# The last 16 columns of V in five loads by rows: a cached attention decode step with a gated mixer MLP

## Chip, cores and metric

The kernel runs on one core of one Trainium2 chip. The metric is device microseconds of one execution of the program: the median of several runs. The profile shows one more execution, taken with the hardware profiler.

## What is computed

Two branches start from the same input x (2 batches, one token, 1024 features), and a gate g = sigmoid(sum(x * gate_w)) mixes them.

```python
# A: one token against a cache of 16384 keys and values, 32 heads of 128
q = (x @ wq)                                     # (2, 32, 1, 128)
scores = einsum("bhqd,bhkd->bhqk", q, k_cache) * (128 ** -0.5)
o = einsum("bhqk,bhkd->bhqd", softmax(scores), v_cache)
a = o.reshape(2, 1, 4096) @ wo
# B: h = gelu(layernorm(x) @ w1), shifted along the sequence, @ w2;
#    x1 = x + hs;  b = x1 + gelu(layernorm(x1) @ w3) @ w4
out = g * a + (1 - g) * b                        # (2, 1, 1024), bf16
```

Everything is bf16 in memory. K and V are 268 MB each, the weights some 36 MB more.

## The kernel before

**Units.** The 32 heads of a batch are taken in 16 pairs, one pair of one batch is a unit, and there are 32 units: `i` counts the pairs, `s` the batches. A unit's K (and later its V) is 8 MB and lies in SBUF as 128 rows of 64 KB: row p holds 256 consecutive cache positions ("columns" of 128 values each, `NJ` = 256), and the first 64 rows belong to one head, the last 64 to the other. `unit_rows` gives that view of the cache in HBM.

**One unit.** POOL spreads the unit's query (L624). DVE transposes the K data in eight chunks (L640), and PE multiplies each with the query (L663) into PSUM. DVE takes the maximum (L647, L649), ACT exponentiates (L685) into `pts`, and PE sums (L704). For the unit before, PE multiplies V with its `pts` (L713, `pv_moving`, 512 values of V at a time moving through PE), DVE adds and scales the parts (L781, L787, `dve_rows`), PE turns them (L731), and after each pair of units PE projects with eight of Wo's slices (L758, `add_rows`).

**Order.** The engines' orders and the semaphores are written out by hand in one critical section. SP issues every large load, all on one queue (q1 in the profile): in the loop K of the unit (L906) when the DVE has transposed enough of the unit before in that cell, V of the unit before (L908) when PE has finished with the V cell, and Wo for a pair (L911). Each `dma_start` raises its semaphore by 16 when it has landed. ACT issues three small loads of four rows each at the start (x and the gate's weights, L82) and the store of the result at the end (L1017), on queue q10.

**The end.** After the loop two units of V remain. SP issues V of the first of them (L934) when the last K data of cell 0 are transposed, and, when PE is done with the V cell, V of the second (L938) in pieces of 128, 64, 48 and 16 columns (`PIECES`), each over all 128 rows. Behind them come the Wo rows of the last two heads in three loads (L946 to L948). PE multiplies the first 192 columns with `pv_moving`; DVE adds the parts; PE puts the result into `last` (L992). The other 64 columns are multiplied the other way round, one column of V at a time as PE's weights and two columns of `pts` moving (L996), piece by piece, with a wait for each piece ahead of its first matmul. DVE scales the sum (L1002), PE projects it with Wo (L758, twelve matmuls, then a wait for the load of L948, then four more), ACT and DVE copy the two halves out of PSUM (L1013, L1015), and ACT stores them (L1017).

The waits that the change touches: the semaphores of these loads were used once before at the kernel's start, so each starts at 16, and `landing(n)` is the value that means that piece n has landed:

```python
for n in range(WIDE, len(PIECES)):
    wait(PE, landed[n + 1], landing(n + 1))
    for _ in range(PIECES[n]):
        ins = PE.matmul(last, lhsT=V[:, j, :], rhs=pts[1][:, j // 4, :, j % 4], ...)
        j += 1
```

Of the kernel before, what the change touches and what calls it, by code (L numbers as in the profile page):

```python
# [88 lines left out]
def kernel(  # L89
# [16 lines left out]
    P = nc.NUM_PARTITIONS  # L106
    B, Sq, D = A_x.shape
    _, H, Sk, Dh = A_k_cache.shape
# [6 lines left out]
    HP = H // 2  # L115
    HALF = P // 2
    NJ = 2 * Sk // P
# [4 lines left out]
    Q4 = 4  # L122
# [19 lines left out]
    def S(name):  # L142
        if name not in sems:
            sems[name] = (tc if name in ("fin", "st") else nc).alloc_semaphore(name)
        return sems[name]
# [59 lines left out]
    def region(cell, elements):  # L205
        return mem[:, cell * CELL : cell * CELL + elements]

    K_CELL = (0, 1)
    V_CELL = 3

    k_rows = A_k_cache.rearrange("b (g t) s d -> b g (t s d)", t=2)
    v_rows = A_v_cache.rearrange("b (g t) s d -> b g (t s d)", t=2)
    wo_rows = A_wo.rearrange("(g p r) n -> g (p r n)", p=WP, r=WR)

    def unit_rows(rows, hp, s):
        if isinstance(hp, int):
            flat = rows[s, hp : hp + 1, :]
        else:
            flat = rows[s, bass.ds(hp, 1), :]
        return flat.rearrange("o (p x) -> (o p) x", p=P)  # L220
# [7 lines left out]
    def wait(engine, name, value):  # L228
        if isinstance(value, int) and value == 0:
            return  # L230
        engine.wait_ge(S(name), value)
# [7 lines left out]
    with tc.tile_critical(no_gpsimd_drain=True):  # L239
        PE, DVE, ACT, POOL, SP = nc.tensor, nc.vector, nc.scalar, nc.gpsimd, nc.sync  # L240
# [10 lines left out]
        for b, row in enumerate((A_x[0, 0], A_x[1, 0], gate_w)):  # L251
# [9 lines left out]
                out=ident_f[:], in_=ident_f[:], compare_op=ALU.not_equal, fill=1.0, base=0,  # L261
# [10 lines left out]
        for k in range(2):  # L272
# [14 lines left out]
                out=lmat[:].rearrange("p (g h k) -> p g h k", h=2, k=4),  # L287
                in_=hm2[:].unsqueeze(1).unsqueeze(3).to_broadcast([P, P // 8, 2, 4]),
# [3 lines left out]
        for h in range(2):  # L292
            at = QP + h * (HB // 2)
# [3 lines left out]
                    out=place[:, at : at + P].rearrange("p (g k) -> p g k", k=2 * QP)[:, :, 0 : HB + 1 : HB],  # L297
                    in_=ident_f[:, h * HALF : (h + 1) * HALF].rearrange("p (g k) -> p g k", k=QP)[:, :, 0:B],
# [6 lines left out]
                out=ident_s[:], in0=ident_f[:], scalar1=-scale, scalar2=None, op0=ALU.mult  # L305
# [6 lines left out]
                out=rep1[:], in_=ident_f[:].rearrange("p (c k) -> p k c", k=QP), axis=AX.X, op=ALU.add  # L312
# [6 lines left out]
                out=mask4[:], in_=ident_f[:].rearrange("p (c k) -> p c k", k=QP), axis=AX.X, op=ALU.add  # L319
# [3 lines left out]
        for g in range(Q4):  # L323
# [3 lines left out]
                    out=rep4[:, g, :].rearrange("p (a k) -> p a k", k=QP),  # L327
# [13 lines left out]
                out=hsel[:], in_=rep1[:, 0:8].rearrange("p (h k) -> p h k", k=4), axis=AX.X, op=ALU.add  # L341
# [179 lines left out]
        def linear(actT, w, R, N, act_key, w_key, banks, out_keys):  # L521
# [7 lines left out]
            def one(n):  # L529
# [19 lines left out]
                out=tsc[:],  # L549
                in_=oacc2[:].rearrange("p a (m k e) -> p (a m) e k", k=QP, e=2),  # L550
# [6 lines left out]
                out=qTb[:], in_=tsc[:].rearrange("p (c k) -> p c k", k=QP)[:, :, 0:B]  # L557
# [15 lines left out]
        for e in range(2):  # L573
# [4 lines left out]
                    out=qd[rows],  # L578
                    in_=R_ps[rows].rearrange("p (hp e v b) -> p e hp b v", e=2, v=4, b=B)[:, e],
# [142 lines left out]
        def v_view(cell):  # L722
            return region(cell, NJ * Dh).rearrange("p (j d) -> p j d", d=Dh)
# [105 lines left out]
        for key in ("qd", "mask4", "qw0", "qw1"):  # L829
# [20 lines left out]
                out=tsc[:, 0:FQ],  # L850
                in_=oacc2[:, :, 0:half].rearrange("p a (i c) -> p c a i", c=FC),
# [34 lines left out]
                out=brow[:], in0=brow[:], scalar1=omgrow[:, 0:1], scalar2=None, op0=ALU.mult  # L886
# [38 lines left out]

        landed = [f"l_{x}" for x in ("wq", "w1", "w2", "xr0", "xr1", "w3", "w4")]

        def landing(n):
            return 32

        PIECES = [128, 64, 48, 16]
        WIDE = 2
        wait(SP, "tr3", 2 * HP)
        SP.dma_start(out=region(0, NJ * Dh), in_=unit_rows(v_rows, HP - 1, 0)).then_inc(S(landed[0]), 16)  # L934
        wait(SP, "pvd", 2 * HP - 1)
        at = 0
        for n, size in enumerate(PIECES):
            SP.dma_start(  # L938
                out=region(V_CELL, NJ * Dh)[:, at * Dh : (at + size) * Dh],
                in_=unit_rows(v_rows, HP - 1, 1)[:, at * Dh : (at + size) * Dh],  # L940
            ).then_inc(S(landed[n + 1]), 16)
            at += size
        wo_heads = A_wo.rearrange("(h d) n -> d h n", d=Dh)
        wo_l = region(2, 2 * D).rearrange("p (e n) -> p e n", e=2)
# [20 lines left out]
                out=rinv2[:], in0=rinv2[:], scalar1=g_rep[:, 1:2], scalar2=None, op0=ALU.mult  # L965
# [14 lines left out]
        V = v_view(V_CELL)  # L980
        moving = sum(PIECES[:WIDE])
        j = 0
        for n in range(WIDE):
            wait(PE, landed[n + 1], landing(n + 1))
            ins = pv_moving(V, 1, j // 4, (j + PIECES[n]) // 4, moving // 4)
            j += PIECES[n]
# [5 lines left out]
        PE.matmul(last, lhsT=red[:, 0, :], rhs=hsel[:], start=True, stop=False)  # L992
# [3 lines that stand above are left out]
                ins = PE.matmul(  # L996
                    last, lhsT=V[:, j, :], rhs=pts[1][:, j // 4, :, j % 4], start=False, stop=(j == NJ - 1)
                )
                j += 1
        ins.then_inc(S("otd"), 1)  # L1000
        wait(DVE, "otd", 2 * HP)
        DVE.tensor_tensor(out=OTl[:, :, HB], in0=last, in1=rinv2[:], op=ALU.mult).then_inc(S("OTd"), 1)  # L1002
        wait(PE, "OTd", 2 * HP)
        wait(PE, landed[-2], landing(-2))
        for h in range(2):
            add_rows(0, OTl, wo_l, h)
# [11 lines left out]
            out=out.rearrange("b s (h g c) -> g (b s) h c", h=2, g=Q4), in_=out_row[0 : P - HB + 1 : HB, :]  # L1018
# [37 lines left out]
```

## Time and profile before

| what | value |
| --- | --- |
| median of 3 runs | 1331.68 us (1331.62 to 1331.88) |
| the profiled execution | 1331.36 us |
| its span in the profile | 1329.6 us |
| granted TensorE clock, mean | 0.803 |
| DMA traffic | 572.68 MB, 431 GB/s over the span |
| PE busy | 826.6 us (62%) |
| DVE busy | 711.4 us (54%) |
| ACT busy | 105.2 us (8%) |

The span runs from the first instruction to the last; the time of the execution is some 2 us longer. PE and DVE are busy for a good half of the span, spread evenly over it; the sixteen DMA engines are busy throughout. Times within the execution are microseconds from the span's start. The loads of the end are issued like this: L934 at 1277.84, the four pieces of L938 from 1294.34 on (1.76 us of SP for the four), then L946 at 1296.15, L947 at 1296.62 and L948 at 1297.10. Each lands some 20 to 30 us after its issue, since all that was issued before it on the queue comes first. A load's bytes are moved as packets, one for a contiguous run of one row, and the trace has a record of each packet (queue, size, start and duration), and of each increment of a load's semaphore.

### The profile page before, as it was taken

How to read it: one execution, taken by the hardware profiler on the slowest of the kernel's cores; microseconds unless marked ns; L12 is line 12 of the kernel's file. 1: busy time of each engine (PE TensorE's matmuls, PEld its weight loads, DVE VectorE, ACT ScalarE, POOL GpSimd, SP SyncE). 2: the span in 40 equal slices, each digit the busy share in tenths (PEclk: the TensorE clock that was granted, in tenths of full speed). 3: DMA queues.
4: the chain of work that ended last, by engine and by line, in shares of the span. 5: the costliest groups of instructions: out<-in, count | busy, mean ns of one | idle time of the engine just before them, and what ended most of it. 6: DMA issues, size and time to landing. Idle time of an engine off the chain costs nothing.

```text
span 1329.6 us, 14078 instructions
## 1 busy us (share of the span) xinstructions
PE 826.6 (62%) x6060; PEld 378.3 (28%) x6060; DVE 711.4 (54%) x712; ACT 105.2 (8%) x165; POOL 15.9 (1%) x47
## 2 busy tenths in 40 slices
PE   2356576565666656567665657656566775656765
PEld 0123232232332323233232323223232322323323
DVE  2365465654556654456565455665455656545561
ACT  0010000000000000000000000000000000000000
POOL 0100000000000000000000000000000000000000
PEclk9677887777888777788877788877788887778886
DMA  9999999999999999999999999999999999999998
GB/s 410 439 420 436 443 426 440 428 430 436 432 436 432 436 430 442 426 442 426 442 426 442 424 442 426 442 426 433 434 430 438 430 436 432 440 428 440 428 440 346
DMA packets 11573, 572.68 MB, mean 431 GB/s; under 512 B 1472, under 2 KB 1740, under 8 KB 1996
## 3 DMA queue, kind: packets, MB, share of 16 engines
q1 hardware_dynamic: 11520, 572.53, 99.6%
q8 instruction: 8, 0.13, 0.0%
q10 hardware_dynamic: 44, 0.01, 0.0%
q14 instruction: 1, 0.01, 0.0%
HBM read 572.53 MB, written 0.00 MB: 431 GB/s over the span
## 4 chain that ended last, share of the span: by engine, by line
DMA 68%; DVE 14%; PE 13%; issue 3%; another core or an unknown queue 1%; POOL 0%; SPq 0%; POOLq 0%; ACT 0%
DMA mem<-in_A_k_cache_dram 66%; DVE kt L640 14%; PE S L663 12%; DMA mem<-in_A_v_cache_dram 2%; PE oacc L713 0%; PE ot L531 0%; SPq L906 0%; PE R L996 0%; POOL qw L267 0%; POOL pt L269 0%; SPq L938 0%; PE arow L758 0%; DVE st L647 0%; POOL ln_rstd L471 0%
## 5 line engine op out<-in xcount | busy, mean ns | idle before, releaser
L663 PE MATMUL S<-kt,qw 128*128 128x512 bf16 x2048 | 552.1, 420 | 261.7 <-DVE kt L640 261.4
L640 DVE STREAM_TRANSPOSE kt<-mem 128x2048 f32<-128x2048 f32 x256 | 571.6, 2284 | 171.1 <-DMA mem<-in_A_k_cache_dram 115.6
L663 PEld LDWEIGHTS S<-kt,qw 128*128 128x128 bf16 x2048 | 197.9, 105 | 602.1 <-issue 301.3
L713 PE MATMUL oacc<-mem,pt 128*8 128x512 bf16 x2032 | 118.3, 386 | 5.7 <-DMA mem<-in_A_v_cache_dram 5.7
L685 ACT ACTIVATE pt<-st,nb 64x256 bf16<-64x256 f32 x64 | 90.1, 1407 | 279.0 <-DVE nb L699 278.5
L731 PE MATMUL ot<-hsel,red 128*128 128x2 f32 x480 | 71.1, 279 | 54.7 <-DVE red L787 54.7
L731 PEld LDWEIGHTS ot<-hsel,red 128*128 128x128 f32 x480 | 68.5, 224 | 69.9 <-DVE red L787 69.9
L781 DVE TENSOR_SCALAR part<-oacc,maskr 128x128 f32<-128x128 f32 x31 | 10.9, 351 | 140.3 <-PE oacc L713 140.3
L674 ACT ACTIVATE Dm<-ident_s,m 128x128 f32<-128x128 f32 x32 | 12.8, 401 | 878.7 <-DVE m L649 878.7
L704 PE MATMUL R<-rs,lmat 128*128 128x1 f32 x64 | 18.4, 357 | 79.1 <-ACT pt L685 79.1
L713 PEld LDWEIGHTS oacc<-mem,pt 128*8 128x8 bf16 x2032 | 46.9, 87 | 64.8 <-DMA mem<-in_A_v_cache_dram 6.8
L708 DVE RECIPROCAL rinv<-R 128x1 f32<-128x1 f32 x32 | 5.4, 168 | 109.6 <-PE R L704 109.5
L647 DVE STREAM_TRANSPOSE st<-S 128x512 f32<-128x512 f32 x32 | 22.9, 717 | 70.1 <-PE S L663 70.1
L676 PE MATMUL R<-Dm,ones_f 128*128 128x128 f32 x64 | 15.6, 326 | 54.4 <-ACT Dm L674 54.4
L814 DVE TENSOR_SCALAR oa<-ot,hm 128x8 f32<-128x8 f32 x30 | 6.8, 226 | 73.9 <-PE ot L731 73.9
L704 PEld LDWEIGHTS R<-rs,lmat 128*128 128x128 f32 x64 | 15.9, 307 | 84.9 <-ACT pt L685 84.7
L758 PE MATMUL arow<-wo,OT 128*17 128x128 bf16 x960 | 28.3, 310 | 10.5 <-DVE OT L819 10.5
L685 ACT ACTIVATION_READ_ACCUMULATOR pt<-st,nb 64x1 f32 x64 | 30.7, 479 | 0.0
L676 PEld LDWEIGHTS R<-Dm,ones_f 128*128 128x128 f32 x64 | 9.5, 188 | 70.3 <-ACT Dm L674 70.3
L758 PEld LDWEIGHTS arow<-wo,OT 128*17 128x17 bf16 x960 | 24.6, 133 | 11.3 <-issue 11.3
L787 DVE SCALAR_TENSOR_TENSOR part<-oacc,maskr,part 128x128 f32<-128x128 f32 x62 | 21.8, 351 | 2.2
L624 POOL TENSOR_TENSOR qw<-qd,mask 128x16 bf16<-128x16 f32 (+1 forms) x32 | 8.3, 262 | 1118.7 <-PE S L663 1118.7
(114 smaller groups left out, 130.0 us busy)
## 6 DMA issues: line engine op xcount, KB each, us to landing
mem<-in_B_w_dram SPq DMA_DIRECT2D x2, 7168.0 KB, 34.4
wo<-in_A_wo_dram SPq DMA_DIRECT2D x15, 512.0 KB, 24.8
mem<-in_B_w_dram SPq DMA_DIRECT2D x2, 2048.0 KB, 28.5
mem<-in_A_v_cache_dram SPq DMA_DIRECT2D x1, 4096.0 KB, 20.8
mem<-in_A_v_cache_dram SPq DMA_DIRECT2D x1, 2048.0 KB, 25.3
mem<-in_A_v_cache_dram SPq DMA_DIRECT2D x1, 1536.0 KB
mem<-in_A_k_cache_dram SPq DMA_DIRECT2D x32, 28.3
mem<-in_A_v_cache_dram SPq DMA_DIRECT2D x1, 512.0 KB
```

The lines of the kernel that those rows point to most:

```text
L640: DVE.transpose(out=kt[n % 2][:], in_=k_view(s)[:, c * CT : (c + 1) * CT, :].rearrange("p j d -> p (j d)").bitcast(FP32),).then_inc(S(f"tr ...
L647: DVE.transpose(out=st[:].rearrange("p j r -> p (j r)"), in_=sps[s][:]).then_inc(S("stT"), 1)
L663: ins = PE.matmul(sps[s][:].rearrange("p (j k) -> p j k", k=QP), lhsT=qw[s][:, v, NG - 1 - m : NG - 1 - m + P], rhs=ktb[:, half * GT : (ha ...
L674: ACT.activation(out=Dm[:], in_=ident_s[:], func=ACTF.Copy, scale=m_t[:, 0:1]).then_inc(S("dm"), 1)
L676: PE.matmul(R_ps[:, 0:P], lhsT=ones_f[:], rhs=Dm[:], start=True, stop=True).then_inc(S("rr"), 1)
L685: ins = ACT.activation(out=pts[s][rows, :, e, :].rearrange("p (m a) k -> p a k m", a=GT // 4), in_=st[rows, :, 0:NG].rearrange("p (a k) m ...
L704: PE.matmul(tot_ps[:, 0:1], lhsT=lmat[:], rhs=rs_t[:], start=True, stop=True).then_inc(S("tt"), 1)
L713: ins = PE.matmul(oacc[s][QP * q : QP * q + 8, :], lhsT=pts[s][:, g].rearrange("p h k -> p (h k)"), rhs=V[:, 4 * g : 4 * g + 4, :].rearran ...
L731: ins = PE.matmul(ot_ps[:, 2 * r : 2 * r + 2], lhsT=red_t[:, r : r + 2 * P - 1 : 2], rhs=hsel[:], start=True, stop=True, skip_group_check= ...
L758: ins = PE.matmul(arow[h][QP * g : QP * g + HB + 1, :], lhsT=o[:, e, :], rhs=w[:, e, at : at + Dh], start=False, stop=stop, skip_group_che ...
L781: ins = DVE.tensor_scalar(out=part[:], in0=in0, scalar1=mask[:, 0:1], scalar2=None, op0=ALU.mult)
L787: ins = DVE.scalar_tensor_tensor(out=red[:] if twice else part[:], in0=in0.unsqueeze(1).to_broadcast([P, 2, Dh]) if twice else in0, scalar ...
```

## The change

The first three pieces of the last unit's V stay as they are. The last piece, 16 columns (4 KB in each row), is no longer one load of 128 rows: it is one load of rows 0 to 111, then four loads of four rows each, 112 to 115, 116 to 119, 120 to 123 and 124 to 127. All five raise the same semaphore, and the wait on PE for this piece asks for 16 * (2 + 4) = 96 instead of 32. The order of the instructions on PE, DVE, ACT and POOL is the same in both kernels; on SP one load has become five, at the same place, with three loads of Wo behind them.

```diff
-        def landing(n):
-            return 32
-
         PIECES = [128, 64, 48, 16]
         WIDE = 2
+        LAST, FEW = len(PIECES) - 1, 4
+        def landing(n):
+            return 16 * (2 + Q4) if n == LAST + 1 else 32
+
         wait(SP, "tr3", 2 * HP)
         SP.dma_start(out=region(0, NJ * Dh), in_=unit_rows(v_rows, HP - 1, 0)).then_inc(S(landed[0]), 16)
         wait(SP, "pvd", 2 * HP - 1)
         at = 0
         for n, size in enumerate(PIECES):
-            SP.dma_start(
-                out=region(V_CELL, NJ * Dh)[:, at * Dh : (at + size) * Dh],
-                in_=unit_rows(v_rows, HP - 1, 1)[:, at * Dh : (at + size) * Dh],
-            ).then_inc(S(landed[n + 1]), 16)
+            cuts = [0] + (list(range(P - Q4 * FEW, P, FEW)) if n == LAST else []) + [P]
+            for first, end in zip(cuts, cuts[1:]):
+                SP.dma_start(
+                    out=region(V_CELL, NJ * Dh)[first:end, at * Dh : (at + size) * Dh],
+                    in_=unit_rows(v_rows, HP - 1, 1)[first:end, at * Dh : (at + size) * Dh],
+                ).then_inc(S(landed[n + 1]), 16)
             at += size
```

## The prediction

> **What bounds the kernel now.** I read the page first. Its busy row of the DMA engines is full in every slice but the last, and the chain that ended last is mostly transfers.
>
> ```profile
> DMA  9999999999999999999999999999999999999998
> ...
> DMA 68%; DVE 14%; PE 13%; issue 3%; another core or an unknown queue 1%; POOL 0%; SPq 0%; POOLq 0%; ACT 0%
> ```
>
> So the kernel streams 572.7 MB at the rate of its sixteen DMA engines. A change to the last load can matter only where that stream runs out, so next comes the timeline of the last 6 us (columns: start, duration, engine, line, operation; in brackets the idle time and what ended it).
>
> ```profile
> 1323.76 1.86 PE L996 MATMUL R<-pt,mem 128*128 128x2 bf16 x64 [0.32 <-DMA mem<-in_A_v_cache_dram]
> 1325.66 0.17 DVE L1002 TENSOR_TENSOR OT_last<-R,rinv_last 128x2 bf16<-128x2 f32 x1 [2.86 <-PE R L996]
> 1325.89 0.22 PEld L758 LDWEIGHTS arow<-mem,OT_last 128*17 128x17 bf16 x12 [0.34 <-DVE OT_last L1002]
> 1325.89 0.72 PE L758 MATMUL arow<-mem,OT_last 128*17 128x128 bf16 x16 [0.26 <-DVE OT_last L1002]
> 1326.32 0.10 PEld L758 LDWEIGHTS arow<-mem,OT_last 128*17 128x17 bf16 x4 [0.21 <-DMA mem<-in_A_wo_dram]
> 1326.44 0.28 ACT L1013 ACTIVATE out_row<-arow 113x128 bf16<-113x128 f32 x1 [24.48 <-PE arow L758]
> ```
>
> Two paths meet at 1326.32. The chain of waits follows one: the 48-column piece of V lands at 1323.72, PE does its 48 and then 16 one-column matmuls (L996) without a gap, DVE scales, PE starts the projection (L758). The other is the last wait, 0.21 us: the last four matmuls wait for the last quarter of Wo (L948). That wait ends last. If it were gone, the four could start at 1326.11, so a gain can be at most **0.21 us**; a delay of L948's landing costs its whole length.
>
> L948 is behind the changed load in the same queue (SP's, q1). The trace keeps, for each load, the times of its sixteen increments, one by each DMA engine. L948's run from 1324.53 to 1326.28: eight engines are done by 1324.84, eight only from 1325.57 on. The windows say the same (the last two columns are DMA share and GB/s).
>
> ```profile
> 1323.00:1324.00 1.00, 0.69 (x11) 0.60 (x12) 0.00 (x0) 0.00 (x0) 0.00 (x0) 0.50 1.02 386
> 1324.00:1325.00 1.00, 1.00 (x44) 1.00 (x41) 0.00 (x0) 0.00 (x0) 0.00 (x0) 0.50 0.56 208
> 1325.00:1326.00 1.00, 0.74 (x32) 0.66 (x29) 0.17 (x1) 0.00 (x0) 0.00 (x0) 0.50 0.36 117
> ```
>
> The reader is to see a stream that ends ragged: full until 1324, half idle after. What counts is the engine that ends last, and the change gives some engines more and others less.
>
> **Which engine is late.** Each engine takes its own packets of q1 one after another, so its lag on the earliest engine can be followed from load to load: within about 0.1 us it stays, except where the engine also carries an instruction fetch (in q8, 16 KB of 948 to 1164 ns each; the first, at 39.24 us, is 8 KB of q14). Seven fetches between 39 and 196 us hit seven different engines, and one at 1310.39 an eighth. At the 64-column piece the lags are 0 to 0.42 us for eight engines and 1.20, 1.48, 1.55, 1.65, 1.71, 1.72, 1.79 and 1.96 us for the others.
>
> **The change, part by part.** *Removed:* a load of 128 rows of 4 KB: eight rows and one increment on each engine. The 128 packets of 4 KB took 159 to 172 ns, median 160. *Added:* 112 rows, which I take as seven per engine, and four loads of four rows. That a four-row load goes to four engines, one row each, is in the trace: ACT's three four-row loads at the start (x and the gate's weights) left 24 packets, 12 rows and 12 increments.
>
> ```profile
> q10 hardware_dynamic: 24, 0.01, 0.1%
> ```
>
> In those records the four engines stand 0, 0.113, 0.268 and 0.286 us apart in each of the three loads, so all three went to the same four. So four engines get 7+4 = 11 rows and five increments, twelve get 7 rows and one.
> - Twelve engines: one row less, **-0.16 us** each.
> - Four engines: 3 x 0.160 + 4 x 0.01 (an increment took 9 ns, the next packet starts about a nanosecond or two later) = **+0.52 us** each.
>
> Are those four early or late ones? The offsets above fit one set of four in the first loads; followed to the end they stand at about 0.23, 0.24, 1.20 and 1.48 us. The first, second and third become 0.75, 0.76 and 1.72, the fourth 1.48 + 0.52 = 2.00. The latest now, 1.96, is not among them and becomes 1.80. The last lag goes from 1.96 to 2.00: **+0.04 us** at L948's landing and so at the end. The weak step is the fourth: near 52 us three engines cross within 12 ns, and it may be its neighbour at 1.55 (then +0.11) or an early one (then the last is 1.80, -0.16).
>
> *Issue on SP.* L938 has four issues more, 0.43 us each and 0.04 between: 4 x 0.47 = 1.9 us, so the three Wo loads (L946 to L948) are issued from 1298.0 instead of 1296.15. Queue q1 has V to move until 1325, which hides this; without that cover it would cost the 1.9 us. Nothing of POOL or ACT is moved past, and SP issues nothing afterwards. If q1 took fewer loads at once than the twelve now outstanding (eight before), SP would stand until the earlier V load lands at 1305.41, still 20 us ahead of need.
>
> *The wait on PE* for the last piece now asks for 96 instead of 32 (16 old, 16 and four times 16 new). Behind it stand 16 matmuls of L996, then DVE's scaling and the projection. The piece landed at 1324.97 and is needed after 48 matmuls of 29 ns, at 1325.16; 0.04 us more stays inside these 0.19. Nothing else on any engine moves: instructions of PE, DVE, ACT and POOL stand in the same order.
>
> **Sum.** The profiled run took 1331.36 us with a span of 1329.6; +0.04 gives 1331.4 for it. It lies 0.3 below the median of the shown runs, 1331.68, so the forecast is 1331.68 + 0.04 = **1331.7 us**: no change that can be seen.
>
> **A price no row shows: four engines writing four neighbouring rows.** Bounds from rows: Wo's 32-row loads in the loop, two rows per engine, had 16 KB packets of 611 to 622 ns, those of 128-row loads 611 at the start: a change of the rows' pattern cost at most 2%, nothing here. From the other side, if the four engines wrote one after another, each row would take four times 160 ns: 4 x 3 x 0.16 = +1.92 us. I take the first, since it is the nearer operation, and since the four are not in step (0.2, 0.2, 1.2, 1.5).
> The Trainium skill, page "SBUF — State Buffer", section "Door 1: The DMA port swizzle", speaks against the change here: four partitions such as 112 to 115 share one port, and bandwidth depends on how many ports are reached. By that rule the sum would be the upper bound; the 611 to 622 ns do not show it, but no load here writes four neighbouring rows alone.
>
> **Rivals.**
> 1. *The extra rows fall on early engines only.* Then the latest lose a row: -0.16 us, 1331.5. For it: half of the engines are early, and two of the four surely so. Against: the third and fourth as followed.
> 2. *The small loads hinder each other.* Pairs in step (the third and fourth are 0.28 us apart, about two rows) would double the four rows' time on a late engine: 0.04 + 4 x 0.16 = +0.68, 1332.4; all four in turn, +1.96, 1333.6. Against: the 611 to 622 ns above.
> 3. *Each small load pays its own round trip in series* (the case on the other side). The only small transfer with both ends in the trace, the 4 KB store, is issued at 1326.98 and lands at 1328.70: 1.72 us. Four in series on the late engine: 6.9 us in place of 0.64, so +6.3, **1338 us**. It decides as soon as an engine waits for the increment of one load before the next one's row: beyond 1326.11 all of it is on the path. Against: the three Wo loads end 0.34 and 0.32 us apart on the last engine, which leaves no room for 1.7 each, and an increment's packet is followed by the next load's packet at once. The Trainium skill, page "DMA: Bandwidth & Descriptors", section "Anatomy of one DMA — SWDGE (gpsimd) path", gives about 2.0 us fixed per DMA, mostly the write's receipt; as an estimate from it four in series would be 8 us. It was fitted on another issuing path, and the 0.34 us apart speak against it in a full queue.
> 4. *It doesn't do what it says:* a four-row load is cut over all sixteen engines. Then the sum of rows is eight for each as before, with four increments more: +0.04, 1331.7, which the time can't tell from the forecast.
>
> **Chances.** Forecast with rival 4: 0.50 (1331.7). Rival 1: 0.25 (1331.5). Rival 2: 0.14 (1332.4 to 1333.6). Rival 3: 0.10 (about 1338). What would be faster by more than the 0.21 us bound has no mechanism here; 0.01. About 0.2% (2.7 us) is what a measurement of this kernel can tell from no change: only rival 3 passes it. So faster 0.01, same 0.89, slower 0.10. The range leaves out rival 3 and the upper half of rival 2. Below it goes to 1331.68 - 0.21, less some 0.3 for the spread of the runs (1331.36 to 1331.88): 1331.1; above to 1332.4 plus the same: 1332.7.
>
> **What would show it.** Right: L996 still 64 matmuls without a gap; sixteen increments of L948 with twelve of them 0.16 us earlier against the 48-column piece and four 0.5 later, the last within 0.2 of before; the wait before the last four of L758 between 0 and 0.4 us. Wrong: a gap inside L996 or a wait of over 1 us for Wo (rival 3), 4 KB packets well over 172 ns (rival 2), a four-row load with other than four rows' packets and four increments (rival 4). An instruction fetch that hits another engine than before would move the lags by 1 us and spoil the sum without being the change's doing.

## The result

The changed kernel takes 1333.41 us (median of 22 runs, 1333.04 to 1334.41) against 1331.63 us (22 runs, 1331.35 to 1331.97): 1.78 us slower, a ratio of 1.0014 (95% interval 1.0008 to 1.0020, which leaves out 1). The prediction's 1331.7 us and its range up to 1332.7 are both below this. The profiled execution has a span of 1331.6 us, 2.0 more than before.

The loss arises in the last 10 us. First the timeline of the changed kernel from the last one-column matmuls on (start, duration, engine, line, operation; in brackets the idle time and what ended it; L999 and L1005 are L996 and L1002 of before).

```profile
1325.36 1.44 PE L999 MATMUL R<-pt,mem 128*128 128x2 bf16 x48 [0.98 <-DMA mem<-in_A_v_cache_dram]
1327.21 0.59 PE L999 MATMUL R<-pt,mem 128*128 128x2 bf16 x16 [0.41 <-DMA mem<-in_A_v_cache_dram]
1327.84 0.17 DVE L1005 TENSOR_TENSOR OT_last<-R,rinv_last 128x2 bf16<-128x2 f32 x1 [4.10 <-PE R L999]
1328.06 0.61 PE L758 MATMUL arow<-mem,OT_last 128*17 128x128 bf16 x16 [0.26 <-DVE OT_last L1005]
```

The 64 matmuls that ran without a gap now stand in two parts. The first 48 start 1.6 us later than before (1325.36 against 1323.76), although their piece of V comes in the same single load as before. The last 16 wait 0.41 us more for the changed piece, whose last increment arrives at 1327.16 instead of 1324.97. The wait before the last four matmuls of L758 is gone: the last load of Wo now lands at 1328.22, just before they need it.

The windows say why. In the last two columns are the DMA engines' busy share and what they moved, in GB/s.

Before, from 1322 to 1323 (the prediction shows the windows from 1323 on):

```profile
1322.00:1323.00 1.00, 0.14 (x1) 0.14 (x1) 0.77 (x2) 0.00 (x0) 0.00 (x0) 0.69 0.98 395
```

and with the change:

```profile
1321.00:1322.00 1.00, 1.00 (x12) 0.11 (x4) 0.00 (x0) 0.00 (x0) 0.00 (x0) 0.50 1.00 360
1322.00:1323.00 1.00, 0.04 (x4) 0.00 (x0) 0.84 (x3) 0.00 (x0) 0.00 (x0) 0.50 1.11 270
1323.00:1324.00 1.00, 0.21 (x1) 0.21 (x2) 0.70 (x2) 0.00 (x0) 0.00 (x0) 0.50 0.94 193
1324.00:1325.00 1.00, 0.38 (x2) 0.29 (x2) 0.00 (x0) 0.00 (x0) 0.00 (x0) 0.50 1.02 206
1325.00:1326.00 1.00, 0.64 (x24) 0.65 (x25) 0.00 (x0) 0.00 (x0) 0.00 (x0) 0.50 0.87 197
1326.00:1327.00 1.00, 0.80 (x30) 0.71 (x27) 0.00 (x0) 0.00 (x0) 0.00 (x0) 0.50 0.70 198
```

Before, the engines moved 386 GB/s from 1323 to 1324 and were half idle after; now they are busy for three microseconds longer at about 200 GB/s. Busy engines that move half as much: the packets themselves are slower. Their records show it. The 128 packets of 4 KB took 160 ns in the median before and 267 now (159 to 458). The slowness is not kept to the changed load: the 12 KB packets of the piece ahead went from 460 to 474 ns to as much as 891, the 2 KB packets of Wo behind it from 84 ns to 135 in the median. All packets of 12 KB and less in this stretch add up to 103.9 us of engine time before and 135.9 after: 32.0 more, or **2.0 us on each of sixteen engines** on average, which is the whole difference of the spans.

The first 12 KB packet of over 500 ns starts at 1321.49, the first 4 KB packet of over 200 ns at 1321.76. In the trace each engine's share of a load ends with a packet for the increment. Between 1321.78 and 1322.77 no increment starts on the queue, and the eight just before are those of the 48-column piece. So no four-row load had begun when the slowness did.

The rows did go where the prediction put them. In the queue's line, from the page,

```profile
q1 hardware_dynamic: 11536, 572.53, 99.6%
```

there are 16 packets more than before's 11520. That is 112 rows with sixteen increments and four times four rows with four increments, 160, in place of 128 and 16, 144.

### The profile page after: what moved, and what is told of

Read it like the earlier page. It is cut to its first block, busy times and chain, and to the rows that moved or that the text cites. A ratio compares the mean times of both kernels' runs of the same rounds, so it can differ in the third digit from the quotient of the medians.

```text
span 1331.6 us, 14082 instructions
## 1 busy us (share of the span) xinstructions
PE 826.1 (62%) x6060; PEld 380.7 (29%) x6060; DVE 710.8 (53%) x712; ACT 105.3 (8%) x165; POOL 15.9 (1%) x47
## 3 DMA queue, kind: packets, MB, share of 16 engines
q1 hardware_dynamic: 11536, 572.53, 99.6%
## 4 chain that ended last, share of the span: by engine, by line
DMA 68%; DVE 15%; PE 12%; issue 3%; another core or an unknown queue 1%; SPq 0%; POOL 0%; POOLq 0%; ACT 0%
DMA mem<-in_A_k_cache_dram 66%; DVE kt L640 15%; PE S L663 12%; DMA mem<-in_A_v_cache_dram 2%; PE ot L531 0%; PE oacc L713 0%; SPq L941 0%; SPq L906 0%; POOL qw L267 0%; POOL pt L269 0%; DVE st L647 0%; POOL ln_rstd L471 0%; PE arow L758 0%; PE R L999 0%
## 5 line engine op out<-in xcount | busy, mean ns | idle before, releaser
L731 PE MATMUL ot<-hsel,red 128*128 128x2 f32 x480 | 75.5, 288 | 54.7 <-DVE red L787 54.7
L731 PEld LDWEIGHTS ot<-hsel,red 128*128 128x128 f32 x480 | 72.9, 236 | 69.9 <-DVE red L787 69.9
L758 PE MATMUL arow<-wo,OT 128*17 128x128 bf16 x960 | 28.3, 310 | 10.5 <-DVE OT L819 10.5
L758 PEld LDWEIGHTS arow<-wo,OT 128*17 128x17 bf16 x960 | 24.6, 132 | 11.3 <-issue 11.3
```

Source lines behind the costliest of these rows:

```text
L731: ins = PE.matmul(ot_ps[:, 2 * r : 2 * r + 2], lhsT=red_t[:, r : r + 2 * P - 1 : 2], rhs=hsel[:], start=True, stop=True, skip_group_check= ...
L758: ins = PE.matmul(arow[h][QP * g : QP * g + HB + 1, :], lhsT=o[:, e, :], rhs=w[:, e, at : at + Dh], start=False, stop=stop, skip_group_che ...
```

## The experiments

The theory after the traces, SPLIT: the load of 112 rows itself is slow, because sixteen engines that share out 112 neighbouring rows write into the same parts of SBUF at once. Its rivals: SMALL (the four-row loads hinder all), SOURCE (the engines meet in HBM), and later COUNT, FIXED (a fixed price for each such load) and SHARES. Each run's time stands beside the kernel before on the same chip. The edits are given in short form, with constants written out as numbers, against the kernel with which the text compares them; the value that PE waits for goes with the number of loads.

**112 rows and 16 rows, no four-row loads.**

```diff
-cuts = [0, 112, 116, 120, 124, 128]
+cuts = [0, 112, 128]
```

> The last piece of V in two loads, rows 0 to 111 and rows 112 to 127 (one row for each engine); no four-row loads. Theory SPLIT (the load of 112 rows is slow itself, since an engine carries seven neighbouring rows, and engines then write into the same groups of rows): most of the loss stays, 1.2 to 2.0 us over before, and 4 KB packets of 230 ns or more in the median. Theory SMALL (the four-row loads on four engines hinder each other and all behind them): within 0.2 us of before and 4 KB packets of 160 to 172 ns.

1333.41 us against 1331.63 (ratio 1.0013, 1.0004 to 1.0023): 1.78 us, exactly the change's loss, with 4 KB packets of 271 ns in the median. SMALL falls as the cause.

**128 rows as before, and four four-row loads behind them.**

```diff
 dma_start(out=V[0:128, piece], in_=v[0:128, piece])
+for first in (112, 116, 120, 124):
+    dma_start(out=spare[first:first + 4], in_=v[first:first + 4, piece])
```

> The last piece of V as before in one load of 128 rows, and behind it four loads of four rows (112 to 127 again) into a spare place of the same rows in SBUF, which nothing reads; PE waits for them too. Theory SPLIT: the 128 rows' packets keep 160 to 172 ns; the added rows cost their engines 0.68 us at 160 ns each and no more than 2.6 us if four engines on one group of four rows write in turn, so 0 to 0.7 us over before, at most 1.5. Theory SMALL: slow packets of 230 ns or more from the four-row loads on, also in the Wo loads behind them, and 1.5 us or more over before.

1332.08 us against 1331.63 (1.0004, 0.9995 to 1.0014): 0.45 us, a quarter of the loss, with 64 KB more to load. The median of the 144 packets is 166 ns, and only the last tenth takes 266 ns or more. That lies in SPLIT's 0 to 0.7 us; SMALL wanted 1.5 us. The four-row loads do slow packets, though: none of the 4 KB packets that start before 1323.12 takes over 172 ns, and the 2 KB packets behind take 98 ns in the median instead of 84.

**The same rows in SBUF from another source.** The last piece is read from w4, with rows 56 KB apart, so the last 16 columns of that unit are not V.

```diff
-in_=unit_rows(v_rows, HP - 1, 1)[first:end, piece]
+in_=w_rows[3][first:end, 0:2048]
```

> As the changed kernel, 112 rows and four times four rows to the same places, but the last piece's bytes are read from the weights w4, rows 56 KB apart, instead of V's rows 64 KB apart, so the last 16 columns of that unit are not V. Theory SPLIT (it lies on SBUF's side or in the split): as the changed kernel, 1.5 to 2.1 us over before, 4 KB packets of 250 ns or so. Theory SOURCE (engines that start seven rows of 64 KB apart in HBM meet there): within 0.3 us of before, 4 KB packets of 160 to 172 ns.

1333.38 us against 1331.63 (1.0014, 1.0004 to 1.0024), packets of 274 ns: as the changed kernel. So it is not V's place in HBM; the rows of the source are neighbours here too.

**Two loads of 64 rows.**

```diff
-cuts = [0, 112, 116, 120, 124, 128]
+cuts = [0, 64, 128]
```

> The last piece of V in two loads of 64 rows, four rows for each engine in each; rows per engine as before, one increment more. If engines lose by writing into the same groups of rows in SBUF (theory SPLIT in its SBUF form: 64 rows reach only half of the groups that 128 do), the 4 KB packets take 250 to 330 ns and the end comes 0.8 to 2.0 us after before's. If the odd number of seven rows for each engine is what is slow, or the source's addresses: 160 to 172 ns and within 0.2 us of before.

1333.64 us against 1331.63 (1.0015, 1.0006 to 1.0025), packets of 260 ns. Neither the odd number of seven rows nor an uneven share is needed for the loss: each engine has eight rows here as before, and loses as much.

That leaves two ways to read it: which rows of SBUF a load writes (GROUPS), or that it is anything else than one load of 128 rows (COUNT). Two kernels with the same number of loads, rows and engines tell them apart.

**Four loads of 32 rows, every fourth row.**

```diff
-rows = slice(0, 128)
+for k in range(4): rows = slice(k, 128, 4)
```

> The last piece in four loads of 32 rows, each taking every fourth row (0, 4, 8, ... then 1, 5, 9, ...): two rows for each engine in each load, eight in all as before. Theory GROUPS (what is slow is that several engines write into the same groups of neighbouring rows of SBUF at once; a load that touches all 32 groups of four rows evenly is not slow): within 0.3 us of before, 4 KB packets of 160 to 175 ns in the median. Theory COUNT (any load of fewer than 128 rows, or several loads in place of one, is slow): 1.2 to 2.5 us over before and 250 ns or more.

1331.59 us against 1331.53 (1.0001, 0.9991 to 1.0010), packets of 159 ns: no loss. **Four loads of 32 neighbouring rows**:

```diff
-for k in range(4): rows = slice(k, 128, 4)
+for k in range(4): rows = slice(32 * k, 32 * k + 32)
```

> The last piece in four loads of 32 neighbouring rows: the same loads, rows per load and rows per engine as with every fourth row. GROUPS: slow, since each load lies in a quarter of the rows: 1.2 to 3.0 us over before and 4 KB packets of 250 ns or more. COUNT: the same as with every fourth row, whatever that gives.

1333.47 us against 1331.53 (1.0015, 1.0005 to 1.0024), packets of 264 ns. In the windows from 1322 to 1325 us, with every fourth row first,

```profile
1322.00:1323.00 1.00, 0.00 (x0) 0.00 (x0) 0.91 (x3) 0.00 (x0) 0.00 (x0) 0.50 0.95 383
1323.00:1324.00 1.00, 0.45 (x2) 0.45 (x3) 0.48 (x1) 0.00 (x0) 0.00 (x0) 0.50 1.04 390
1324.00:1325.00 1.00, 1.00 (x39) 1.00 (x40) 0.00 (x0) 0.00 (x0) 0.00 (x0) 0.50 0.59 216
```

and then with 32 neighbouring rows,

```profile
1322.00:1323.00 1.00, 0.00 (x0) 0.00 (x0) 0.93 (x3) 0.00 (x0) 0.00 (x0) 0.50 0.92 221
1323.00:1324.00 1.00, 0.30 (x2) 0.30 (x2) 0.61 (x2) 0.00 (x0) 0.00 (x0) 0.50 0.92 211
1324.00:1325.00 1.00, 0.28 (x2) 0.20 (x1) 0.00 (x0) 0.00 (x0) 0.00 (x0) 0.50 1.03 242
```

the reader is to see, in the first two windows, about the same busy share and little more than half the bytes; in the third the spread loads are nearly through. COUNT falls.

**Two loads of 64 rows, even and odd.**

```diff
-cuts = [0, 64, 128]
+for k in range(2): rows = slice(k, 128, 2)
```

> The last piece in two loads of 64 rows, the even and the odd ones: four rows for each engine in each load. GROUPS: 4 KB packets of 160 to 200 ns and within 0.4 us of before, against 260 ns and 2.0 us over before for two loads of 64 neighbouring rows. COUNT: as two loads of 64 neighbouring rows.

1331.54 us against 1331.53 (1.0001, 0.9991 to 1.0011), packets of 159 ns, where 64 neighbouring rows took 260 ns and 2.0 us.

**The first piece, 32 KB in each row, in 112 and 16 rows**; the last piece as before.

```diff
-PIECES[0]: rows 0:128
+PIECES[0]: rows 0:112, 112:128
```

> The last piece in one load as before; instead the first piece (128 columns, 32 KB in each row) comes in two loads, rows 0 to 111 and 112 to 127. GROUPS: the loss is a lower rate, so it grows with the bytes: the 128 packets of 32 KB take 1.8 to 2.0 us in place of 1.215, which is some 75 to 100 us of engine time or 5 to 6 us for each of sixteen, and their neighbours some more: 5 to 12 us over before. If the loss were a fixed price for each such load (theory FIXED): 1.2 to 2.0 us over before as with 16 columns.

1343.51 us (4 runs, 1342.39 to 1344.96) against 1331.53 (1.0088, 1.0071 to 1.0105): 12.0 us, at the top of what GROUPS allowed, and FIXED falls. The packets of 32 KB took 2274 ns in the median instead of 1215, more than the 1.8 to 2.0 us expected, and up to 4834; those of the next piece, an ordinary load of 128 rows, up to 2794 instead of 622. Two windows of before,

```profile
1310.00:1315.00 5.00, 1.06 (x18) 0.39 (x6) 1.70 (x5) 0.00 (x0) 0.00 (x0) 1.00 0.95 403
1315.00:1320.00 5.00, 3.25 (x32) 0.94 (x32) 0.00 (x0) 0.00 (x0) 0.00 (x0) 0.66 0.98 418
```

and those of this kernel's profiled execution, at 1344.96 us the slowest of the four:

```profile
1305.00:1310.00 5.00, 3.06 (x32) 1.05 (x36) 0.00 (x0) 0.00 (x0) 0.00 (x0) 0.50 1.08 242
1310.00:1315.00 5.00, 2.96 (x42) 1.05 (x34) 1.70 (x5) 0.00 (x0) 0.00 (x0) 0.89 1.10 285
1315.00:1320.00 5.00, 0.00 (x0) 0.00 (x0) 0.00 (x0) 0.00 (x0) 0.00 (x0) 0.79 1.20 203
1320.00:1325.00 5.00, 0.00 (x0) 0.00 (x0) 0.00 (x0) 0.00 (x0) 0.00 (x0) 0.50 0.83 98
1325.00:1330.00 5.00, 1.15 (x12) 0.39 (x16) 0.00 (x0) 0.00 (x0) 0.00 (x0) 0.50 0.79 226
```

The stream runs at 200 to 285 GB/s up to 1320. From 1320 to 1325 it sinks to 98: only seven of the 32 KB packets begin there, and they take 4301 ns in the median. They come last, so some must be of rows 112 to 127; the records don't name rows, so that sixteen neighbours are worse than 112 is likely and not shown. The packets of the stretch add up to 599.8 us against 380.3, 13.7 more for each engine; the span grew by 13.5.

**The shares of the changed kernel, but spread rows.** Four engines get 11 rows and twelve get 7, as in the changed kernel, by eight loads none of which takes neighbouring rows.

```diff
-rows = slice(0, 128)
+three loads slice(k, 128, 4), k = 0, 1, 2; one slice(3, 128, 8);
+four loads slice(f, f + 25, 8), f = 7, 39, 71, 103
```

> The last piece so that each engine has the share that the changed kernel gives it (four engines 11 rows, twelve engines 7), but no load of neighbouring rows: three loads of 32 rows (every fourth row from 0, 1 and 2), one load of 16 rows (3, 11, 19, ...) and four loads of four rows each, eight rows apart (7, 15, 23, 31 and so on). Theory GROUPS: the prediction's sum, which reckoned with full rate, then holds: 0.2 us below to 0.3 us above before, 4 KB packets of 160 to 180 ns in the median. Rival SHARES (the four-row loads or the uneven shares cost by themselves, hidden behind the slow large load in the changed kernel): 0.5 to 2 us over before.

1331.90 us (11 runs, 1331.75 to 1332.08) against 1331.64 (27 runs, 1331.23 to 1332.00; ratio 1.0002, 0.9993 to 1.0011): the medians are 0.26 us apart, inside what GROUPS expected, though the packets, 185 ns in the median (159 to 251), were a little slower than it said. So uneven shares and four-row loads cost about that much when their rows are spread, and not 1.8 us. Which of the eight loads slows the packets from 160 to 185 ns was not tried.

**SBUF's rows or the source's?** Between neighbouring and spread rows both sides changed. Two kernels part them; in both, V's rows come into wrong places in the last 16 columns.

```diff
-for k in range(4): out rows slice(k, 128, 4),        source rows slice(k, 128, 4)
+for k in range(4): out rows slice(32*k, 32*k + 32),  source rows slice(k, 128, 4)
```

> Four loads of 32 neighbouring rows in SBUF, each filled from every fourth row of the source, so that the last 16 columns of the unit are rows of V in the wrong places. GROUPS on SBUF's side: slow, 1.5 to 2.3 us over before, 4 KB packets of 250 ns or more. If the source's rows decide: within 0.3 us of before and 160 to 175 ns.

1333.39 us against 1331.64 (1.0013, 1.0004 to 1.0022), packets of 260 ns. And the other way round:

```diff
+for k in range(4): out rows slice(k, 128, 4),        source rows slice(32*k, 32*k + 32)
```

> The other way round: every fourth row in SBUF, filled from 32 neighbouring rows of the source (again V's rows in the wrong places). GROUPS on SBUF's side: within 0.3 us of before, 160 to 175 ns. If the source's rows decide: 1.5 to 2.3 us over before and 250 ns or more.

1331.64 us against 1331.64 (0.9999, 0.9990 to 1.0008), packets of 159 ns. For loads of 32 rows it is SBUF's rows, then, and not the source's; for the load of 112 rows this pair was not run.

## Why the prediction was wrong

- *That the stream of loads bounds the kernel and only its end counts, that the last wait was for L948's load, and that at most 0.21 us could be gained:* held. What was lost is engine time of the same stream, 2.0 us for each engine.
- *The engines' shares, 7 and 11 rows, one row of a four-row load on each of four engines:* the counts agree: 11536 packets, and 32 increments of the changed piece, sixteen and four times four. That all four small loads go to the same four engines was not followed. The spread kernel laid out for these shares behaves much as the sum said (+0.04 reckoned, 0.26 between medians).
- ***"Twelve engines: one row less, -0.16 us each" and "Four engines: 3 x 0.160 + 4 x 0.01 = +0.52 us each":* this step failed.** It counted the difference in rows at the 160 ns of a load of 128 rows and let all other packets keep their time. The 4 KB packets took 267 ns, and packets of the loads ahead and behind slowed with them: +32.0 us of engine time where the sum had 12 x (-0.16) + 4 x 0.52 = +0.16. The error is a duration taken from a row of the same size but another shape of load.
- *The price no row shows:* it asked about neighbouring rows, but only for the sixteen rows of the four-row loads and not for the 112. And it leaned on the wrong row: the Wo loads of the loop, 611 to 622 ns, take every fourth row, the pattern of 32 rows that is not slow in the experiments. The pair of 32-row kernels (159 ns against 264) shows that this row had nothing to say about neighbouring ones.
- *Rival 2, the small loads hinder each other, up to 1333.6:* close in its number by luck, and wrong in its place. Without any four-row load the loss is the same 1.78 us; four-row loads behind a load of 128 rows cost 0.45.
- *Rival 3, a round trip for each small load, 1338 us:* did not happen; eight loads in place of one cost 0.26 us.
- *Rival 1, -0.16 us, and rival 4, sixteen engines for a four-row load:* the first was not seen in any run; the second is excluded by the packet count.
- *The wait on PE for 96, the four issues on SP:* SP spent 3.16 us on eight issues in place of 1.76 on four, which put the issue of the Wo loads 1.4 us further behind that of the first piece (1.9 reckoned) and cost nothing, as reckoned. That the last piece stays inside 0.19 us of slack did not hold, for the reason above.
- *Which engine is last:* the step that was called weak (the fourth engine at 1.48 or 1.55) never came to decide anything.

The Trainium skill, page "SBUF — State Buffer", section "Door 1: The DMA port swizzle", has the rule that fits: rows 0 to 63 of SBUF reach no more ports than rows 0 to 31, so 64 rows load no faster than 32. The runs agree: 260 ns with 64 neighbouring rows, 264 with 32. By the same map 112 rows still reach all sixteen ports, so this count of ports alone does not give 267 ns for them. That two or more engines stand on one port at a time, since seven neighbouring rows run over two or three groups of four, is argued and not shown: the trace does not say which engine wrote which row. The Trainium skill says further, on the same page, section "Can I just issue two DMAs to hit both halves?", that only one transfer spanning all 128 partitions reaches all ports. Read as a load of all 128 rows this does not hold here: four loads of 32 rows, each spread over the 128, ran at 159 ns.

Two things stay open: by what mechanism the load of 112 rows is slow, and why the packets of whole loads ahead and behind slow down so much (12 KB up to 891 ns, 16 KB up to 2794). That engines still or already in those loads write to the parts on which the others crowd would explain it; no run tried it.

## What to carry to other kernels

The time of a DMA packet belongs to the rows of SBUF that the load writes, not only to its size: take it from a load with the same set of rows. Without such a row the bound must be wide: in the slow loads here the median was 1.6 to 1.9 times that of a load of 128 rows, and single packets took up to four times as long. If a load has to be cut by rows, cut it so that each part is spread over all 128 rows (every second, every fourth), rather than into blocks of neighbours; four blocks of 32 cost 1.9 us for half a megabyte here, four times every fourth row nothing that could be measured. In a kernel that lives on its DMA stream, a slow load at one place is paid at the end in full, by the loads around it too.

## What the runs showed of the hardware

- A load of 112, 64 or 32 neighbouring rows out of the 128 takes the sixteen engines together down to a half to two thirds of their rate (190 to 250 GB/s instead of 390), though all of them are busy.
- The slowness reaches into ordinary loads of 128 rows on the same queue, the one ahead (12 KB packets, up to 891 ns instead of 474) as well as the one behind (16 KB, up to 2794 instead of 622).
- Each instruction fetch of 16 KB (948 to 1164 ns) sets one DMA engine back by about a microsecond, and in this stream, which never runs dry, the lag stays. In the kernel before, each load's increments show it: two engines are late in the load that lands at 51 us, one more after each fetch, seven from 203 us on and still seven in L934's load at 1304. The fetch at 1310.39 makes eight; they are 1.20 to 1.96 us behind the earliest at the 64-column piece.
